# One group of products with v for each unit, and w2 loaded, measured and split by groups of its own

## The chip, the cores and the metric

The kernel runs on one NeuronCore of a Trainium2 chip. The metric is the time of one execution on the device in microseconds (us), and a kernel's time is the median over its runs. Beside it stands the profile of one execution: every instruction of TensorE (PE, with its weight loads as PEld), VectorE (DVE), ScalarE (ACT), GpSimd (POOL) and of the queue on SyncE that issues the DMAs (SP), with start, length and what released it.

## What is computed

A block of a transformer over 2048 tokens of width 512: a layer norm, then attention with a sliding window (32 heads of width 16, window 256) and beside it a SwiGLU network of inner width 1792; their product is added to the input. All inputs and the output are float32.

```python
B, S, D = 1, 2048, 512        # H = 32, Dh = 16, W = 256, F = 1792
xn = _layernorm(x, axis=-1)

qkv = (xn @ wqkv).reshape(B, S, 3, H, Dh).transpose(2, 0, 3, 1, 4)
q, k, v = qkv[0], qkv[1], qkv[2]
scores = jnp.einsum("bhqd,bhkd->bhqk", q, k) * (Dh ** -0.5)
mask = (idx[:, None] - idx[None, :] >= 0) & (idx[:, None] - idx[None, :] < W)
p = _softmax(jnp.where(mask[None, None], scores, -1e9), axis=-1)
o = jnp.einsum("bhqk,bhkd->bhqd", p, v)
s = o.transpose(0, 2, 1, 3).reshape(B, S, D) @ wo

h = _silu(xn @ w1) * (xn @ w3)
g = _silu(h @ w2)
return x + s * g
```

## The kernel before

**Precision.** Large products run in float16, each float32 operand split into a high and a low half after a scaling by powers of two, so that one product is three matmuls (high by high, high by low, low by high). Each weight is measured first: sums of squares by rows on ACT or DVE (`squares`, L222), a small matmul with ones that sums them over the partitions, and some ten small DVE instructions that turn the sum into a power of two (`powers`, L250). Then `split_pool` (L302) makes the halves: ACT scales the raw tile in place (L303) and casts the high half (L304), POOL subtracts twice for the low half (L300).

**Tiles.** The tokens are cut into four tiles `t` of 512. The attention of a tile is done for four groups `g` of eight heads, each in two passes `p`: 32 **units** (t, g, p). The network of a tile runs over 14 blocks `f` of 128 inner columns: `gate_up` (products with w1 and w3, L836) and, after each of the four groups of blocks in `GROUPS` (f 0 to 3, 4 to 7, 8 to 10, 11 to 13), `down` (products with w2, L881). The weights are split during tile 0 and written to DRAM (`dW1`, `dW2`), from where the later tiles load them.

**A unit.** A first pass over a unit's scores (`pass1`, L588), made two units ahead, gives the row maxima: VectorE reads each pair of score tiles with its mask and keeps the maximum (the `junk` instructions, L600). Call one such row M if its scores lie in one of the two double banks of the pool `pss` (tile `s`), and X if they lie in `po`, the one double bank of the pool `pso`. The second pass (`pass2`) makes the scores once more, turned, in five chunks (four in tile 0): a W row is one chunk's score matmuls into `s` (L662), DVE adds the mask (L669), ACT takes the exponential into a float32 tile `pt` (L672). The products of `pt` with v (L690, called V here) gather all chunks in `po`; at the unit's end ACT copies one half of `po` to `os` (L700) and DVE adds the other (L703), and only then is `po` free for the next X.

**Order.** TensorE's order is the order in which the code is written; on the other engines a scheduler sets the order by priorities, and each engine takes its list in order. `PLAN` and `FIRST_PLAN` (L1020, L1021) give a unit's five batches of rows: "WMX" is a W, an M and an X row, and the numbers behind it are the chunks whose products with v follow. `spread` (L1052) puts the dense matmuls (network, projections) between the batches, by their cost in matmuls of 512 columns; a chunk's products with v count `COLS` = 2.5. `later(n, f)` makes `f` n steps on, a step being a batch or a piece of some six dense matmuls; `beside_scores` hangs a small product onto one of the next M or X rows.

**Slots.** Raw weights, halves and the tiles of the network live in 41 slots of 2 KB per partition, which `take` and `give` hand round, the longest free first. In tile 0 `load(0, f)` (L762 to L766) loads w1, w3 and w2 of a block together, five blocks ahead (`LEAD`); `measure` (L770) takes two blocks with their six tiles at once; `measure_down` (L803) at a group's end only combines the powers already found (`p132`) and lets `cut` split the raw w2 tiles, which have lain in their slots since.

Of the kernel before, what the change touches and what calls it, by code (L numbers as in the profile page):

```python
# [10 lines left out]
F32 = mybir.dt.float32  # L11
BF16 = mybir.dt.bfloat16
# [9 lines left out]
P = 128  # L22
# [29 lines left out]
SLOTS = 41  # L52
# [26 lines left out]
def tile_block(ctx: ExitStack, tc: tile.TileContext, x, wqkv, wo, w1, w3, w2, out):  # L79
# [15 lines left out]
    ppool = pool("ppool", 4)  # L95
# [656 lines left out]
    p132 = const.tile([P, FB], F32, name="p132")  # L752
    down_scale = const.tile([P, len(GROUPS)], F32, name="dsc")

    def load(t, f):
        if t:
            WF[t, f] = a, b = [take(F16) for _ in range(2)], take(F16)
            for k in range(2):
                nc.sync.dma_start(a[k], dW1[f, k])
            nc.sync.dma_start(b, dW2[f])  # L760
            return
        RAW[f] = raw, raw2 = [take(F32) for _ in range(2)], take(F32)  # L762
        for k, w in enumerate((w1, w3)):
            nc.sync.dma_start(raw[k].rearrange("p (c f) -> p c f", f=P),
                              w[:, f * P:(f + 1) * P].rearrange("(c p) f -> p c f", p=P))
        nc.sync.dma_start(raw2, w2[f * P:(f + 1) * P, :])  # L766
# [3 lines left out]
    def measure(f, apart=0):  # L770

        raws = [RAW[f + i][0] for i in range(2)]
        sb = squares([raws[0][0], raws[1][0], raws[0][1], raws[1][1], RAW[f][1], RAW[f + 1][1]], on_act=6 if f > 2 else 4, apart=apart)

        def scale(s=None):
            pp = small.tile([P, 3, 2], F32, name="pp")
            pi = small.tile([P, 3, 2], F32, name="pi")
            return then(s, powers(sb, 6, pp.rearrange("p a b -> p (a b)"), pi.rearrange("p a b -> p (a b)"), s),
                        lambda: rest(pp, pi))

        def rest(pp, pi):
# [21 lines left out]
    def measure_down(k):  # L803

        f0, f1 = GROUPS[k]
        n = f1 - f0
        q = small.tile([P, 1], F32, name="q")
        nc.vector.tensor_reduce(q, p132[:, f0:f1], axis=AX.X, op=ALU.max)
        nc.vector.tensor_scalar(down_scale[:, k:k + 1], q, 1.0 / (HS * WS), None, op0=ALU.mult)
        nc.vector.reciprocal(q, q)  # L810
        sw = small.tile([P, 4], F32, name="sw2")
        nc.vector.tensor_scalar(sw[:, 0:n], p13[:, f0:f1], q, WS, op0=ALU.mult, op1=ALU.mult)

        def cut(f):
            raw2 = RAW.pop(f)[1]
            WF[0, f][1] = b = take(F16)
            split_pool(b[:, 0:D], b[:, D:], raw2, sw[:, f - f0:f - f0 + 1])
            give(raw2, after=5)
        assert measured >= set(range(f0, f1))
        for i, f in enumerate(range(f0, f1)):  # L820
            later(1 + 2 * i, lambda f=f: cut(f))
# [137 lines left out]
    def feed_forward():  # L959
# [3 lines left out]
        for t in range(NT):  # L963
            for f in range(FB):
                if t == 0:
                    if f % 2 or f == 0:
                        pieces += [(0, lambda f=f: load(0, f)) for f in (range(f + LEAD, min(f + LEAD + 2, FB)) if f else range(4, LEAD + 1))]
# [275 lines left out]
```

## Time and profile before

| | |
|---|---|
| runs shown | 861.09, 861.37, 858.77 us; median 861.09 |
| the profiled execution: its own time | 861.01 us |
| the profiled execution: span from first to last instruction | 859.2 us |
| busy: DVE, ACT, POOL | 608.3 us (71%), 407.9 us (47%), 198.0 us (23%) |
| granted TensorE clock, mean over the span | 0.992 |

The busy time of an engine is the time in which at least one of its instructions ran. In a timeline a row gives start, length, engine, source line, operation, what is written and read, and a count; the bracket at the end tells how long the engine was idle ahead of it and what ended the wait. In the list of waits the three numbers are the total, the count and the longest.

### The profile page before, as it was taken

Reading aid. Unit: us, or ns where it says so; the run is one execution under the profiler, and the core shown is the slowest. Engines: PE = TensorE matmul, PEld = TensorE weight load, DVE = VectorE, ACT = ScalarE, POOL = GpSimd, SP = SyncE. Lnnn points to the kernel's source line nnn. Section 1 sums busy time; section 2 is a strip of 40 time slices with the busy share of each in tenths; the row PEclk is TensorE's granted clock in tenths of the full one; section 3 lists DMA queues with packets and bytes.
Section 4 is the critical chain, followed back from the end, with each engine's and each line's share of the span. In section 5 each row is a group of like instructions: output and inputs, shape, how many; then the busy total and the mean of one; then the engine's idle time right before and its main releaser. Section 6 shows DMA issues by size and latency. Waiting matters only on the chain.

```text
span 859.2 us, 22511 instructions
## 1 busy us (share of the span) xinstructions
PE 820.9 (96%) x8734; PEld 380.0 (44%) x8734; DVE 608.3 (71%) x2013; ACT 407.9 (47%) x598; POOL 198.0 (23%) x325
## 2 busy tenths in 40 slices
PE   9899888899999999998999999999999999999998
PEld 4344334444444444443444444444444444444444
DVE  8786656976787667797777876677676787675435
ACT  6898776273426444344343445443443444433521
POOL 2254256151113203111111112120211113031211
PEclk9999899999999999999999999999999999999999
DMA  9958446236643443452533432534442353333201
GB/s 303 292 195 258 144 143 183 74 101 193 174 121 89 116 118 110 147 151 64 132 104 86 144 104 80 164 118 106 143 128 89 102 153 84 112 102 90 62 13 59
DMA packets 95323, 110.62 MB, mean 129 GB/s; under 512 B 17200, under 2 KB 60528, under 8 KB 95216
## 3 DMA queue, kind: packets, MB, share of 16 engines
q1 hardware_dynamic: 94928, 108.67, 43.5%
q8 instruction: 68, 1.11, 0.6%
q10 hardware_dynamic: 288, 0.52, 0.2%
q14 instruction: 39, 0.32, 0.1%
HBM read 76.28 MB, written 28.57 MB: 122 GB/s over the span
## 4 chain that ended last, share of the span: by engine, by line
PE 57%; DVE 15%; issue 7%; DMA 7%; ACT 7%; POOL 4%; SPq 3%; DVEq 0%; POOLq 0%; ACTq 0%
PE m L836 20%; PE m L881 12%; PE po L690 6%; PE m L534 6%; DVE junk L600 5%; PE m L923 3%; POOL slot L300 3%; PE s L662 3%; PE m L504 3%; DVE s L669 2%; PE s L588 2%; ACT pt L672 1%; DMA slot<-in_A_x_dram 1%; DMA dr<-dd 1%; SPq L734 1%
## 5 line engine op out<-in xcount | busy, mean ns | idle before, releaser
L300 POOL TENSOR_TENSOR slot<-slot,slot 128x256 f16<-128x256 f32 (+1 forms) x228 | 149.5, 681 | 568.1 <-ACT slot L860 446.2
L836 PE MATMUL m<-XH,slot 128*128 128x512 f16 x896 | 267.5, 380 | 2.7 <-DVE slot L851 1.9
L672 ACT ACTIVATE pt<-s,es 128x1024 f32<-128x1024 f32 x152 | 167.8, 1113 | 198.9 <-DVE s L669 186.4
L836 PEld LDWEIGHTS <-slot 128*128 128x128 f16 x1344 | 125.1, 98 | 158.5 <-issue 16.3
L836 PE MATMUL m<-XL,slot 128*128 128x512 f16 x448 | 169.8, 379 | 0.0
L881 PE MATMUL m<-slot,slot 128*128 128x512 f16 x672 | 159.5, 387 | 3.1 <-DVE slot L851 1.9
L600 DVE CUSTOM_DVE_ANT_0 junk<-s,MW 128x320 bf16<-128x320 f32 x288 | 139.6, 485 | 30.8 <-PE s L588 20.1
L669 DVE TENSOR_TENSOR s<-s,MK 128x256 f32<-128x256 f32 (+2 forms) x280 | 118.8, 434 | 55.3 <-PE s L662 51.1
L881 PEld LDWEIGHTS <-slot 128*128 128x128 f16 x672 | 63.1, 99 | 84.0 <-issue 14.4
L690 PE MATMUL po<-pt,V 64*32 64x320 f32 (+4 forms) x2880 | 84.8, 345 | 1.3 <-ACT pt L672 1.1
L600 DVE CUSTOM_DVE_ANT_0 junk<-po,MW 128x320 bf16<-128x320 f32 x160 | 77.3, 483 | 6.7 <-DVE M L600 0.5
L860 ACT CAST slot<-slot 128x512 f16<-128x512 f32 x56 | 34.6, 618 | 74.9 <-DVE slot L856 72.8
L851 DVE SCALAR_TENSOR_TENSOR slot<-slot,m 128x512 f32<-128x512 f32 x56 | 38.4, 685 | 32.1 <-ACT slot L847 32.0
L690 PEld LDWEIGHTS po<-pt,V 64*32 64x32 f32 x2880 | 47.1, 106 | 30.8 <-issue 5.5
L662 PE MATMUL s<-qa,KA 50*64 50x320 f16 (+3 forms) x1472 | 58.0, 259 | 1.7 <-ACT pt L672 0.9
L847 ACT ACTIVATE slot<-m,sgs 128x512 f32<-128x512 f32 x56 | 38.3, 683 | 41.8 <-PE m L836 39.7
L662 PEld LDWEIGHTS <-KA 50*64 50x64 f16 x1472 | 32.6, 105 | 56.4 <-issue 36.1
L588 PE MATMUL s<-KA,qa 48*64 48x320 f16 (+2 forms) x648 | 46.5, 299 | 6.5 <-DVE M L600 3.6
L856 DVE SCALAR_TENSOR_TENSOR slot<-m,slot 128x512 f32<-128x512 f32 x56 | 38.4, 686 | 17.9 <-PE m L836 17.3
L897 DVE SCALAR_TENSOR_TENSOR slot<-m,dsc,slot 128x512 f32<-128x512 f32 x48 | 35.7, 745 | 20.0 <-PE m L881 19.9
L588 PEld LDWEIGHTS <-qa 48*64 48x64 f16 x1024 | 29.6, 106 | 39.8 <-issue 26.6
L534 PE MATMUL m<-XH,whi 128*128 128x512 f16 x120 | 45.5, 387 | 1.6 <-DVE slot L897 0.9
(151 smaller groups left out, 880.7 us busy)
## 6 DMA issues: line engine op xcount, KB each, us to landing
slot<-dW SPq DMA_DIRECT2D x126, 256.0 KB
slot<-in_B_w_dram SPq DMA_DIRECT2D x42, 256.0 KB
dW<-slot SPq DMA_DIRECT2D x42, 256.0 KB
slot<-in_A_x_dram SPq DMA_DIRECT2D x30, 256.0 KB
KA<-dK SPq DMA_DIRECT2D x24, 288.0 KB
qa<-dQ SPq DMA_DIRECT2D x32, 192.0 KB
dK<-slot SPq DMA_DIRECT2D x16, 256.0 KB
dQ<-slot SPq DMA_DIRECT2D x16, 256.0 KB
```

Of the source, the lines that this page charges most:

```text
L300: op(out[:, c], a[:, c], b[:, c])
L534: nc.tensor.matmul(cell["pp"], a[:, k, c, :], b[:, c, :], start=(c, i) == parts[0][0], stop=(c, i) == parts[-1][-1])
L588: nc.tensor.matmul(s[64 * c:64 * c + 64, r, :n], qa[rows, 2 * p + a, ii * P + 64 * c:ii * P + 64 * c + 64], ka[rows, 2 * p + a, e - n:e], ...
L600: nc.vector.tensor_tensor_reduce(out=junk[:, :n], in0=s[:, r, :n], in1=mask, scale=1.0, scalar=NEG, op0=ALU.add, op1=ALU.max, accum_out=M[ ...
L662: nc.tensor.matmul(s[64 * h:64 * h + 64, r, o:o + 64 * n], ka[rows, 2 * p + a, 64 * (m + 4):64 * (m + 5)], qa[rows, 2 * p + a, 64 * (m + k ...
L669: nc.vector.tensor_add(v, v, MK[:, kind, of:of + n, :].unsqueeze(1).to_broadcast([P, 2 * len(which), n, 64]))
L672: nc.scalar.activation(pt, s, AF.Exp, scale=es)
L690: nc.tensor.matmul(cell["po"][32 * i:32 * i + 32, h, 64 * (m + k):64 * (m + k + n)], V[64 * h:64 * h + 64, (4 * t + m // 2) % VB, hd * VW: ...
L836: nc.tensor.matmul(cell[k], w[:, (a * NC + c) * P:(a * NC + c + 1) * P], b[:, c, :], start=c == 0 and i == 0, stop=c == NC - 1 and i == 2)
L851: nc.vector.scalar_tensor_tensor(sg, sg, 1.0, cell[0], op0=ALU.add, op1=ALU.mult)
L856: nc.vector.scalar_tensor_tensor(sg, cell[1], 0.5 * HS / (WS * XS)**2, sg, op0=ALU.mult, op1=ALU.mult)
L881: nc.tensor.matmul(ps, hh[:, a * TW + b * P:a * TW + (b + 1) * P], w[:, c * D:(c + 1) * D], start=f == f0 and i == 0, stop=f == f1 - 1 and ...
```

## The change

1. **The plans.** All products with v of a unit now stand in its fifth batch. The X rows move from the first three batches to the second, third and fourth, the two W rows of one batch from the third to the fourth. As all five `pt` tiles live until then, their pool gets a fifth buffer, and `SLOTS` falls from 41 to 39.
2. **w2 in tile 0.** `load` takes w1 and w3 alone. w2 has its own `load_down`, two blocks ahead of the block that is being computed, and `measure_down` is called for each block: ACT squares the raw tile (L814), and with the last block of a group follow the cast, the small matmuls beside a row of scores, the powers and the cuts. `measure` now has four tiles instead of six. Of the first two pairs of blocks two squares each go to DVE as before, now those of w3.

```diff
-SLOTS = 41
+SLOTS = 39
-    ppool = pool("ppool", 4)
+    ppool = pool("ppool", 5)
...
-        RAW[f] = raw, raw2 = [take(F32) for _ in range(2)], take(F32)
+        RAW[f] = raw = [take(F32) for _ in range(2)]
...
-        nc.sync.dma_start(raw2, w2[f * P:(f + 1) * P, :])
...
-        sb = squares([raws[0][0], raws[1][0], raws[0][1], raws[1][1], RAW[f][1], RAW[f + 1][1]], on_act=6 if f > 2 else 4, apart=apart)
+        sb = squares([raws[0][0], raws[1][0], raws[0][1], raws[1][1]], on_act=4 if f > 2 else 2, apart=apart)
...
-            nc.vector.tensor_mul(p132[:, ff], p13[:, ff], pp[:, 2, :])
...
+    def load_down(f):
+        RAW2[f] = raw = take(F32)
+        nc.sync.dma_start(raw, w2[f * P:(f + 1) * P, :])
+
+    def measure_down(k, f):
...
+        nc.scalar.activation(sq, RAW2[f], AF.Square, accum_out=NORMS[k][:, f - f0:f - f0 + 1])
+        if f < f1 - 1:
+            return
+        sb = small.tile([P, n], BF16, name="sb2")
+        nc.vector.tensor_copy(sb, NORMS[k])
...
+            return then(s, powers(sb, n, p2, small.tile([P, n], F32, name="pi2"), s), lambda: rest(p2))
...
+            for i, f in enumerate(range(f0, f1)):
+                later(1 + 2 * i, lambda f=f: cut(f))
+        beside_scores(2, scale)
...
-                    pieces += [(0, lambda k=k: measure_down(k)) for k, (_, f1) in enumerate(GROUPS) if f == f1 - 1]
+                    pieces += [(0, lambda f=f: load_down(f)) for f in range(f + 2 if f else 0, min(f + 3, FB))]
+                    for m in range(f + 1 if f else 0, min(f + 2, FB)):
+                        k = next(k for k, (_, f1) in enumerate(GROUPS) if m < f1)
+                        pieces.append((0, lambda k=k, m=m: later(2, lambda: measure_down(k, m))))
...
-    FIRST_PLAN = (("WMX", ()), ("WMX", ()), ("WMX", ()), ("WM", (0, 1)), ("M", (2, 3)))
-    PLAN = (("WMX", ()), ("WMX", ()), ("WWX", ()), ("WM", (0, 1, 2)), ("MM", (3, 4)))
+    FIRST_PLAN = (("WM", ()), ("WMX", ()), ("WMX", ()), ("WMX", ()), ("M", (0, 1, 2, 3)))
+    PLAN = (("WM", ()), ("WMX", ()), ("WMX", ()), ("WWX", ()), ("MM", (0, 1, 2, 3, 4)))
...
-    LAST_PLANS = ((("LW", ()), ("WW", ()), ("WW", (0, 1, 2)), ("", (3, 4))),
-                  (("WW", ()), ("WW", ()), ("W", (0, 1, 2)), ("", (3, 4))))
+    LAST_PLANS = ((("LW", ()), ("WW", ()), ("WW", ()), ("", (0, 1, 2, 3, 4))),
+                  (("WW", ()), ("WW", ()), ("W", ()), ("", (0, 1, 2, 3, 4))))
```

What this does to the order of instructions is shown at three places. The first is **TensorE in the fourth batch of the unit (t, g, p) = (1, 2, 0)**; `pt_5703` and `pt_5779` are the second and third of its five chunks (each of the rows stands there twice and is shown once). Before, dense matmuls (L504, values for the next tile) follow the third chunk:

```order
L690 MATMUL po_5875<-pt_5703,V_139 32x320 x2
L690 MATMUL po_5875<-pt_5779,V_139 32x320 x2
L690 MATMUL po_5875<-pt_5703,V_139 32x192 x2
L690 MATMUL po_5875<-pt_5779,V_139 32x192 x2
L504 LDWEIGHTS XH_3565
L504 MATMUL m1_5900<-wvh_466,XH_3565 128x512
```

Of the change, the same unit in its fifth batch; `pt_5742` and `pt_5826` are now the second and third chunk, `pt_5903` and `pt_5920` the fourth and fifth:

```order
L690 MATMUL po_5983<-pt_5742,V_139 32x320 x2
L690 MATMUL po_5983<-pt_5826,V_139 32x320 x2
L690 MATMUL po_5983<-pt_5742,V_139 32x192 x2
L690 MATMUL po_5983<-pt_5826,V_139 32x192 x2
L690 MATMUL po_5983<-pt_5903,V_139 32x320 x2
L690 MATMUL po_5983<-pt_5920,V_139 32x320 x2
```

The dense matmuls between the two groups have moved ahead of the first; the matmuls of V themselves and their order are the same.

The second place is **VectorE from the end of that unit**: L703 is the addition that frees `po`, and the first `junk` that reads `po` behind it belongs to the next unit's first X row (rows that only read out the accumulator are left out). Before:

```order
L703 TENSOR_TENSOR os_5966<-os_5966,po_5875 128x512
L927 SCALAR_TENSOR_TENSOR slot24_5977<-m0_5976,us_4192,slot24_5977 128x512
L669 TENSOR_TENSOR s_5997<-s_5997,MK_119 128x4x2x64
L600 ISA junk_6014,M_5996<-s_6009,MW_111 128x320
L600 ISA junk_6016,M_5996<-s_6009,MW_111 128x320
L600 ISA junk_6025,M_5996<-po_6018,MW_111 128x320
```

Of the change:

```order
L703 TENSOR_TENSOR os_6032<-os_6032,po_5983 128x512
L947 SCALAR_TENSOR_TENSOR slot25_5954<-m0_5953,us_4227,slot25_5954 128x512
L669 TENSOR_TENSOR s_6053<-s_6053,MK_119 128x4x2x64
L600 ISA junk_6070,M_6052<-s_6065,MW_111 128x320
L600 ISA junk_6072,M_6052<-s_6065,MW_111 128x320
L547 SCALAR_TENSOR_TENSOR slot9_6092<-m1_6079,slot9_6092 128x512
L669 TENSOR_TENSOR s_6108<-s_6108,MK_119 128x4x64
L600 ISA junk_6128,M_6052<-s_6121,MW_111 128x320
L669 TENSOR_TENSOR s_6108<-s_6108,MK_119 128x2x2x64
L600 ISA junk_6130,M_6052<-s_6121,MW_111 128x320
L621 CAST mt_6132<-s_6121 32x128
L600 ISA junk_6143,M_6052<-po_6138,MW_111 128x320
```

A whole batch (a W and an M row, with its dense matmuls) now lies between the freeing of `po` and the next row that needs it. On TensorE the dense matmuls between V and the next X were 12 for most units (9 to 15 over all); now there are 6 (3 to 9), the batch "WM" and 15 or 18 more. Between the batch "WWX" and the next rows, which need the banks of its two W rows, there were 12 in ten of the 22 units that have such a batch (15 to 24 in the others); now there are 18 in 19 of them (15, 21 and 24 in the others).

The third place is **ScalarE around the end of the first unit, (0, 0, 0)**. L231 are squares of w1 and w3, L814 (L231 with six tiles before) those of w2, L894 and L914 the first evictions of `down`, L700 the copy that frees `po`. Before:

```order
L231 ACTIVATE sqa_1975,ssq_1909<-slot18_1583 128x512
L700 COPY os_1486<-po_1408 128x512
L303 ACTIVATE slot38_745<-slot38_745,sw2_1915 128x512
L231 ACTIVATE sqa_1990,ssq_1909<-slot13_1589 128x512
L303 ACTIVATE slot5_751<-slot5_751,sw2_1915 128x512
L894 ACTIVATE slot3_1509<-m1_1496,dsc_156 128x512
L231 ACTIVATE sqa_2002,ssq_1909<-slot25_1584 128x512
L303 ACTIVATE slot8_828<-slot8_828,sw2_1915 128x512
L672 ACTIVATE pt_1535<-s_1522,es0_355 128x1024
```

Of the change:

```order
L814 ACTIVATE sqa_1632,ssq2_1172<-slot22_1260 128x512
L231 ACTIVATE sqa_1643,ssq_1576<-slot28_1096 128x512
L231 ACTIVATE sqa_1653,ssq_1576<-slot19_1100 128x512
L814 ACTIVATE sqa_1787,ssq2_1172<-slot12_1578 128x512
L231 ACTIVATE sqa_1974,ssq_1924<-slot30_1568 128x512
L700 COPY os_1495<-po_1458 128x512
L231 ACTIVATE sqa_1984,ssq_1924<-slot9_1572 128x512
L814 ACTIVATE sqa_1987,ssq2_1986<-slot8_1722 128x512
L914 ACTIVATE slot36_1511<-m1_1440,dsc_155 128x512
L231 ACTIVATE sqa_2004,ssq_1924<-slot17_1569 128x512
L672 ACTIVATE pt_1537<-s_1524,es0_346 128x1024
```

The splits of w2's second group (L303 with `sw2`) have gone from here to a later place, and squares whose tiles come by DMA stand closer together ahead of the copy, the eviction and the next exponential.

More of the change, by code (lines that the diff above doesn't have):

```diff
@@ L751, in tile_block @@
     p13 = const.tile([P, FB], F32, name="p13")
-    p132 = const.tile([P, FB], F32, name="p132")
     down_scale = const.tile([P, len(GROUPS)], F32, name="dsc")
@@ L765, in load @@
                               w[:, f * P:(f + 1) * P].rearrange("(c p) f -> p c f", p=P))
-        nc.sync.dma_start(raw2, w2[f * P:(f + 1) * P, :])
     measured = set()
     def measure(f, apart=0):
-        raws = [RAW[f + i][0] for i in range(2)]
-        sb = squares([raws[0][0], raws[1][0], raws[0][1], raws[1][1], RAW[f][1], RAW[f + 1][1]], on_act=6 if f > 2 else 4, apart=apart)
+        raws = [RAW.pop(f + i) for i in range(2)]
+        sb = squares([raws[0][0], raws[1][0], raws[0][1], raws[1][1]], on_act=4 if f > 2 else 2, apart=apart)
         def scale(s=None):
-            pp = small.tile([P, 3, 2], F32, name="pp")
-            pi = small.tile([P, 3, 2], F32, name="pi")
-            return then(s, powers(sb, 6, pp.rearrange("p a b -> p (a b)"), pi.rearrange("p a b -> p (a b)"), s),
+            pp = small.tile([P, 2, 2], F32, name="pp")
+            pi = small.tile([P, 2, 2], F32, name="pi")
+            return then(s, powers(sb, 4, pp.rearrange("p a b -> p (a b)"), pi.rearrange("p a b -> p (a b)"), s),
                         lambda: rest(pp, pi))
@@ L801, in measure, with scale, rest, cut @@
             later(10 if apart else 6, scale)
-    def measure_down(k):
+    RAW2 = {}
+    NORMS = {}
+    def load_down(f):
+        RAW2[f] = raw = take(F32)
+        nc.sync.dma_start(raw, w2[f * P:(f + 1) * P, :])
+    def measure_down(k, f):
         f0, f1 = GROUPS[k]
         n = f1 - f0
[L807 to L821, printed above, removed]
+        if f == f0:
+            NORMS[k] = small.tile([P, n], F32, name="ssq2")
+        sq = ppool.tile([P, D], BF16, name="sqa", bufs=1)
+        nc.scalar.activation(sq, RAW2[f], AF.Square, accum_out=NORMS[k][:, f - f0:f - f0 + 1])
[3 more added lines that the diff above has]
+        nc.vector.tensor_copy(sb, NORMS[k])
+        def scale(s):
+            p2 = small.tile([P, n], F32, name="pp2")
+            return then(s, powers(sb, n, p2, small.tile([P, n], F32, name="pi2"), s), lambda: rest(p2))
+        def rest(p2):
+            assert measured >= set(range(f0, f1))
+            nc.vector.tensor_mul(p2, p2, p13[:, f0:f1])
+            q = small.tile([P, 1], F32, name="q")
+            nc.vector.tensor_reduce(q, p2, axis=AX.X, op=ALU.max)
+            nc.vector.tensor_scalar(down_scale[:, k:k + 1], q, 1.0 / (HS * WS), None, op0=ALU.mult)
+            nc.vector.reciprocal(q, q)
+            sw = small.tile([P, 4], F32, name="sw2")
+            nc.vector.tensor_scalar(sw[:, 0:n], p13[:, f0:f1], q, WS, op0=ALU.mult, op1=ALU.mult)
+            def cut(f):
+                raw = RAW2.pop(f)
+                WF.setdefault((0, f), [[None, None], None])[1] = b = take(F16)
+                split_pool(b[:, 0:D], b[:, D:], raw, sw[:, f - f0:f - f0 + 1])
+                give(raw, after=5)
+            for i, f in enumerate(range(f0, f1)):
+                later(1 + 2 * i, lambda f=f: cut(f))
+        beside_scores(2, scale)
@@ L965, in feed_forward @@
                 if t == 0:
[L966 to L967 removed]
+                    if (f % 2 or f == 0) and f + LEAD < FB - 2:
+                        pieces += [(0, lambda f=f: load(0, f)) for f in (range(f + LEAD, f + LEAD + 2) if f else range(4, LEAD + 1))]
+                    elif f + LEAD == FB - 1:
+                        pieces += [(0, lambda f=f: load(0, f)) for f in range(FB - 2, FB)]
                     if f % 2 and f + 3 < FB:
                         pieces.append((0, lambda f=f + 3: measure(f, 1)))
[L970 removed]
+                    pieces += [(0, lambda f=f: load_down(f)) for f in range(f + 2 if f else 0, min(f + 3, FB))]
+                    for m in range(f + 1 if f else 0, min(f + 2, FB)):
+                        k = next(k for k, (_, f1) in enumerate(GROUPS) if m < f1)
+                        pieces.append((0, lambda k=k, m=m: later(2, lambda: measure_down(k, m))))
                 else:
```

2 lines of the change are left out of this document (1 added, 1 removed).

## The prediction

> **What bounds the kernel now.** First the page's busy times, then the windows that cut the span into long stretches, with the granted clock in the third column from the end.
>
> ```profile
> span 859.2 us, 22511 instructions
> PE 820.9 (96%) x8734; PEld 380.0 (44%) x8734; DVE 608.3 (71%) x2013; ACT 407.9 (47%) x598; POOL 198.0 (23%) x325
> ```
>
> ```profile
> 94.10:100.90 6.80, 6.17 (x24) 2.34 (x25) 2.55 (x14) 4.47 (x10) 0.01 (x1) 0.50 0.40 138
> 152.10:155.50 3.40, 3.40 (x10) 1.20 (x9) 3.40 (x13) 1.00 (x1) 0.00 (x0) 0.50 0.18 44
> 391.00:394.40 3.40, 3.40 (x10) 1.21 (x8) 2.45 (x10) 1.11 (x1) 1.24 (x2) 0.50 0.25 72
> 200.00:400.00 200.00, 193.49 (x2158) 89.70 (x2159) 149.10 (x494) 82.64 (x105) 35.87 (x54) 0.99 0.46 129
> 400.00:600.00 200.00, 197.01 (x2360) 92.68 (x2362) 145.39 (x462) 83.39 (x102) 33.29 (x50) 1.00 0.41 114
> 600.00:800.00 200.00, 197.46 (x2194) 91.11 (x2187) 139.17 (x436) 83.47 (x101) 35.95 (x54) 1.00 0.38 110
> ```
>
> TensorE is the bound: busy for 820.9 of 859.2 us, and for 588 of the 600 us from 200 to 800. Only three things can move the end much: its work, its 38 us of idle time, and the three stretches in which it was granted half the clock (6.8 + 3.4 + 3.4 us, so some 6.8 us lost). The idle time is uneven: 12 us between 200 and 800, and most of the rest in the first 200, where the weights are split. The list of waits, whole, then for the first 200 us, then for what follows, names what bears on this change:
>
> ```profile
> PE po L588 <- DVE os L703: 9.0, 8, 3.8
> PE s L588 <- ACT pt L672: 2.1, 5, 0.7
> PE po L690 <- ACT pt L672: 1.1, 1, 1.1
> ...
> PE po L588 <- DVE os L703: 5.9, 3, 3.8
> ...
> PE po L588 <- DVE os L703: 3.1, 5, 1.2
> ```
>
> The largest wait of all is an X row that needs `po` while the unit before it is still being copied out of it.
>
> **The products with v in one group.** The timeline of TensorE, rows of three places in units of tile 1, the third a view of the end of one group:
>
> ```profile
> 378.22 0.31 PE L588 MATMUL s<-KA,qa 48*64 48x320 f16 x4
> 378.46 1.53 PE L690 MATMUL po<-pt,V 64*32 64x256 f32 x48
> ...
> 401.18 0.31 PE L588 MATMUL po<-KA,qa 48*64 48x320 f16 x4
> 401.42 0.39 PE L836 MATMUL m<-XH,slot 128*128 128x512 f16 x1
> ...
> 405.69 0.53 PE L690 MATMUL po<-pt,V 64*32 64x192 f32 x16
> ...
> 405.86 0.37 PE L690 MATMUL po<-pt,V 64*32 64x192 f32 x8
> 406.16 0.39 PE L923 MATMUL m<-slot,slot 128*128 128x512 f16 x1
> ```
>
> From the last M row to V it takes 0.24 us from start to start, and from the last such row to a dense matmul 0.24 us as well. So the fourth batch, which loses its V, saves nothing at the front. It saves the way out: one pass of eight V matmuls follows the pass before it after 0.17 us, but a dense matmul follows the last pass after 0.30 us. Where V goes on into V, 0.13 us goes. That is once for each of 32 units: **-4.2 us**. The matmuls of V themselves are the same in number, size and order, so nothing else of their time changes. The lower bound of this term is nothing, if the next fetch of weights fills the gap again; the upper bound is the whole 0.30 us, 9.6 us. I take the measured difference.
>
> [...]
>
> **The wait for `po`.** How it arises, once in a quiet place and once in tile 0:
>
> ```profile
> 264.63 1.07 PE L690 MATMUL po<-pt,V 64*32 64x320 f32 x32
> ...
> 268.32 0.41 PE L662 MATMUL s<-qa,KA 50*64 50x256 f16 x8
> 268.56 0.31 PE L588 MATMUL s<-KA,qa 48*64 48x320 f16 x4
> 270.08 0.33 PE L588 MATMUL po<-KA,qa 48*64 48x320 f16 x4 [1.21 <-DVE os L703]
> ```
>
> ```profile
> 148.79 0.62 ACT L304 CAST slot<-slot 128x512 f16<-128x512 f32 x1 [2.65 <-POOL slot L300]
> 149.32 0.72 ACT L303 ACTIVATE slot<-slot,sw 128x512 f32<-128x512 f32 x1
> 149.94 0.56 ACT L700 COPY os<-po 128x512 f32<-128x512 f32 x1
> ```
>
> In the first, V starts at 264.63, and the X row could have started at about 268.87, that is 4.2 us later with 12 dense matmuls between; it had to wait to 270.08. In the second the copy out of `po` stood behind a cast that itself waited 2.65 us for POOL, and TensorE lost 3.8 us. After the change 6 dense matmuls, a batch "WM" and 18 more follow V. A dense matmul takes 0.22 us (401.42 and its like), so V's end to the next X grows from about 3.2 us to 24 x 0.22 + 2 x 0.6 = 6.5 us, by 3.3 us. The longest of these eight waits is 3.8 us, the next 1.4. I count all eight as gone: **-9.0 us**. What comes late next at these places is the W or M row of the same batch, which waits for its bank in `s`; it does not need `po`. The lower bound is what the part from 200 us on holds, 3.1 us, if each wait of the first 200 us is taken over by another engine's lateness.
>
> **The rows behind two W rows.** The five waits of an M row for the exponential look like this:
>
> ```profile
> 282.36 0.42 PE L662 MATMUL s<-qa,KA 50*64 50x320 f16 x12
> 283.12 0.33 PE L588 MATMUL s<-KA,qa 48*64 48x320 f16 x4 [0.34 <-ACT pt L672]
> ```
>
> The M row takes over the bank of the second of two W rows a batch earlier, 12 dense matmuls (2.6 us) away. Now 18 lie there in nearly all units, 1.3 us more than before, and no wait of this kind was longer than 0.7 us: **-1.9 us** of the 2.1. V itself needs the fifth exponential one batch later than its scores, as before.
>
> **The clock.** Two of the three stretches at half clock start right behind a wait for `po`: that at 152.1 behind the one of 3.8 us, that at 391.0 behind one of 0.7 us which closes a row of three. Without them the clock should stay: 3.4 x 0.5 for each, **-3.4 us**. The first, at 94.1, follows a wait of 2.9 us for a maximum (L600), and I leave it in.
>
> [...]
>
> **w2 on its own.** The work is the same: as many squares, casts and subtractions, the same DMAs. On ACT it is the groups
>
> ```profile
> L231 ACT ACTIVATE sqa<-slot 128x512 bf16<-128x512 f32 x48 | 30.1, 628 | 6.0 <-DMA slot<-in_B_w_dram 4.7 <-DMA slot<-in_A_wqkv_dram 0.9
> L304 ACT CAST slot<-slot 128x512 f16<-128x512 f32 x46 | 27.2, 614 | 4.5 <-POOL slot L300 3.0 <-PE m L881 1.0 <-PE s L662 0.3
> ```
>
> with the same counts. What is added: four groups of small matmuls beside a row of scores, and about ten small DVE instructions for each, less the seven multiplications that go.
>
> ```profile
> 60.78 0.18 PE L263 MATMUL s<-sb,onesb 64*64 64x6 bf16 x4
> 60.81 0.31 PE L588 MATMUL s<-KA,qa 48*64 48x320 f16 x4
> ...
> L275 DVE TENSOR_SCALAR al<-al 128x6 int32<-128x6 int32 (+1 forms) x13 | 2.6, 197 | 0.1
> ```
>
> The next row of scores starts 0.03 us behind such a group of four, so TensorE pays 0.1 us, **+0.2** with the entry. DVE pays 4 x 10 x 0.2 - 7 x 0.2 = 6.6 us, spread over 180 us in which it is busy about 70% of the time; its idle time hides it, and without that cover all 6.6 would show. What is moved is the danger: a square stands in ACT's list ahead of evictions and exponentials, and ACT takes its list in order. One case is in the trace:
>
> ```profile
> 114.42 0.63 ACT L231 ACTIVATE sqa<-slot 128x512 bf16<-128x512 f32 x1 [3.81 <-DMA slot<-in_B_w_dram]
> ...
> 115.05 1.09 ACT L672 ACTIVATE pt<-s,es 128x1024 f32<-128x1024 f32 x1
> ...
> 116.20 1.05 PE L690 MATMUL po<-pt,V 64*32 64x320 f32 x28 [1.09 <-ACT pt L672]
> ```
>
> ACT waited 3.8 us for a weight, the exponential behind it came late, TensorE lost 1.1 us. Now ten of the fourteen w2 tiles (f 4 to 13) are loaded about one and a half blocks ahead of their square, some 8 us by 24 dense matmuls a block, and queue on SP behind writes of split weights that wait for POOL. In the third place of the order shown, seven such squares stand ahead of an eviction that TensorE's next bank waits for. Against that, the loads at the start are fewer by a third, and w2 no longer holds its slots from five blocks ahead, so that w1 and w3 come earlier. The bounds are from a gain of 1.1 us (the old case gone) to ten times 1.1 us; near to the one row there is, two such stalls of about 1.1 us: **+2.3 us**. The fifth `pt` buffer and the two slots fewer I cost at nothing: tiles 1 to 3 load two blocks ahead, about 10 us.
>
> **The sum** is made against the profiled execution's own time, 861.0 us (its span, and 1.8 us around it), which is within 0.1 us of the median of the runs shown, 861.1: 861.0 - 4.2 - 9.0 - 1.9 - 3.4 + 0.2 + 2.3 = **845.0 us**.
>
> **The rivals.**
>
> *The first 200 us give it back.* There DVE, ACT and POOL set the pace in turns, and TensorE, let go at one place, stops at the next: the list above has `po` waiting for `os` with 5.9 us there, but also the 2.9 us wait for a maximum. Then the 5.9 us and the stretch at 152.1 stay: 845.0 + 5.9 + 1.7 = 852.6 us. For it speaks that the longest wait came from POOL, which keeps its work; against it that the waits go away by 3.3 us of distance, whoever causes them.
>
> *Nothing is gained.* V now needs the last two exponentials at once, and the row behind it follows sooner (6 dense matmuls). If TensorE waits 0.35 us for `pt` in each of 24 units, 8.4 us more come to 852.6: 861.0 us. For it speaks that such waits of 0.2 to 0.7 us exist; against it that they arise behind 12 dense matmuls and now have 18.
>
> *Slower: ACT held by w2.* If each of the ten late tiles stops ACT for 3.8 us as in the row above, and TensorE, which takes up the freed `s` and `m` banks within about 1 us, loses 2.8 of it, that is 28 us, and two more drops of the clock, 3.4: 845.0 - 2.3 + 31.4 = 874 us. It decides from about 1.8 us of loss for each tile, where the 18 us of the other terms are used up. Against it: in the trace ACT waited only twice for a weight, 4.7 us in all, though w2 then queued in the same list.
>
> [...]
>
> **How the numbers follow.** The unknown terms at their low ends (9.6 us for V, 1.1 us gained on w2) give 845.0 - 5.4 - 3.4 = 836.2 us, at their high ends (nothing for V, 11 us lost on w2) 845.0 + 4.2 + 8.7 = 857.9. All of them at one end is unlikely, so the forecast's own range is 838 to 851, and it has 0.62. The first rival, 851 to 857, has 0.21; the second, within 0.3% (2.6 us, about what a measurement of this kernel can tell from no change), 0.08; the third 0.09. So faster 0.83, same 0.08, slower 0.09. The range from 837 to 857 leaves out the last two, 0.17, and a little below.
>
> **What would show it.** In the profile after, "PE po <- DVE os" should be gone from the list of waits, and "PE s <- ACT pt" with it but for some tenths. V should stand in one row of about 2.5 us in each unit of tiles 1 to 3, against 1.46 and 1.19. TensorE's busy time should fall by about 4 us and half of the clock's 3.4, its idle time to about 29 us. The windows from 200 to 800 should have at most 7 us of idle time. If I am wrong, ACT's list will show L814 waiting for DMAs by more than 5 us, or the first `down` of tile 0 waiting for its w2 halves, or the half clock will be granted at new places.

## The result, and the profile after

The changed kernel takes **838.58 us** (median of 4 runs, 837.43 to 839.88) against 860.56 us for the kernel before, measured beside it: a ratio of 0.975, 95% interval 0.972 to 0.977. The forecast was 845.0 us, its range 837 to 857. The direction and the range held; the time is 6.4 us below the forecast.

The page of the profiled execution (its own time 837.43 us), and the windows of the changed kernel with the granted clock in the third column from the end:

```profile
span 835.6 us, 22584 instructions
PE 809.6 (97%) x8750; PEld 381.5 (46%) x8750; DVE 614.4 (74%) x2034; ACT 408.2 (49%) x598; POOL 196.7 (24%) x325
```

```profile
200.00:400.00 200.00, 196.73 (x2300) 93.67 (x2299) 156.08 (x514) 89.65 (x116) 42.27 (x64) 1.00 0.46 135
400.00:600.00 200.00, 199.56 (x2306) 94.65 (x2304) 149.66 (x473) 85.08 (x105) 34.75 (x53) 1.00 0.43 119
600.00:800.00 200.00, 199.24 (x2285) 93.66 (x2289) 137.69 (x413) 85.24 (x104) 38.42 (x58) 1.00 0.36 102
92.30:95.70 3.40, 3.40 (x9) 1.21 (x8) 2.05 (x11) 3.34 (x7) 0.00 (x0) 0.50 0.44 156
```

The span is 23.6 us shorter. Of that, TensorE's busy time gave 11.3 us (820.9 to 809.6) and its idle time 12.3 us (38.3 to 26.0). From 200 to 800 us only 4.5 us of idle time are left, from 12.0. One stretch at half clock remains, the last row.

The list of waits of the changed kernel, its head; `po <- os` is nowhere in it:

```profile
PE s L588 <- DVE M L600: 4.0, 2, 2.9
PE m L856 <- DVE slot L547: 2.5, 3, 1.3
PE po L588 <- DVE XL L472: 1.9, 2, 1.1
PE s L588 <- ACT pt L672: 1.9, 3, 0.7
```

### The profile page after: what moved, and what is told of

The parts are those of the page before. It is cut to its first block, busy times and chain, and to the rows that moved or that the text cites. A ratio compares the mean times of both kernels' runs of the same rounds, so it can differ in the third digit from the quotient of the medians.

```text
span 835.6 us, 22584 instructions
## 1 busy us (share of the span) xinstructions
PE 809.6 (97%) x8750; PEld 381.5 (46%) x8750; DVE 614.4 (74%) x2034; ACT 408.2 (49%) x598; POOL 196.7 (24%) x325
## 4 chain that ended last, share of the span: by engine, by line
PE 68%; DVE 9%; issue 7%; DMA 6%; ACT 5%; POOL 3%; SPq 2%; POOLq 0%; ACTq 0%; DVEq 0%
PE m L856 24%; PE m L901 13%; PE po L690 8%; PE m L534 6%; PE s L662 5%; PE m L943 4%; PE m L504 3%; POOL slot L300 3%; DVE junk L600 2%; PE s L588 2%; DMA slot<-in_B_w_dram 2%; DMA qa<-dQ 1%; DVE s L669 1%; PE po L588 1%; ACT slot L303 1%
## 5 line engine op out<-in xcount | busy, mean ns | idle before, releaser
L856 PEld LDWEIGHTS <-slot 128*128 128x128 f16 x1344 | 124.8, 98 | 159.9 <-issue 17.7
L600 DVE CUSTOM_DVE_ANT_0 junk<-s,MW 128x320 bf16<-128x320 f32 x276 | 134.3, 486 | 24.7 <-PE s L588 15.7
L901 PEld LDWEIGHTS <-slot 128*128 128x128 f16 x672 | 62.5, 98 | 82.2 <-issue 12.3
L600 DVE CUSTOM_DVE_ANT_0 junk<-po,MW 128x320 bf16<-128x320 f32 x172 | 83.7, 487 | 5.6 <-DVE al L272 0.4
L690 PE MATMUL po<-pt,V 64*32 64x320 f32 (+4 forms) x2880 | 77.7, 343 | 0.5 <-DVE pp L277 0.5
L690 PEld LDWEIGHTS po<-pt,V 64*32 64x32 f32 x2880 | 51.9, 106 | 24.1 <-PE s L588 4.7
L871 DVE SCALAR_TENSOR_TENSOR slot<-slot,m 128x512 f32<-128x512 f32 x56 | 38.3, 684 | 28.0 <-ACT slot L867 27.0
L662 PEld LDWEIGHTS <-KA 50*64 50x64 f16 x1472 | 30.2, 105 | 55.7 <-issue 36.1
L876 DVE SCALAR_TENSOR_TENSOR slot<-m,slot 128x512 f32<-128x512 f32 x56 | 38.5, 688 | 12.3 <-PE m L856 11.4
L534 PE MATMUL m<-XL,whi 128*128 128x512 f16 x120 | 44.5, 379 | 0.0
```

Source lines behind the costliest of these rows:

```text
L534: nc.tensor.matmul(cell["pp"], a[:, k, c, :], b[:, c, :], start=(c, i) == parts[0][0], stop=(c, i) == parts[-1][-1])
L600: nc.vector.tensor_tensor_reduce(out=junk[:, :n], in0=s[:, r, :n], in1=mask, scale=1.0, scalar=NEG, op0=ALU.add, op1=ALU.max, accum_out=M[ ...
L662: nc.tensor.matmul(s[64 * h:64 * h + 64, r, o:o + 64 * n], ka[rows, 2 * p + a, 64 * (m + 4):64 * (m + 5)], qa[rows, 2 * p + a, 64 * (m + k ...
L690: nc.tensor.matmul(cell["po"][32 * i:32 * i + 32, h, 64 * (m + k):64 * (m + k + n)], V[64 * h:64 * h + 64, (4 * t + m // 2) % VB, hd * VW: ...
L856: nc.tensor.matmul(cell[k], w[:, (a * NC + c) * P:(a * NC + c + 1) * P], b[:, c, :], start=c == 0 and i == 0, stop=c == NC - 1 and i == 2)
L876: nc.vector.scalar_tensor_tensor(sg, cell[1], 0.5 * HS / (WS * XS)**2, sg, op0=ALU.mult, op1=ALU.mult)
```

## The experiments

All times are medians beside the kernel before on the same chip; the ratio is to that kernel. "The change" means the changed kernel. The profiled executions took their medians within 2 us, but for that of e4 (847.87 against 844.91).

### The two parts apart

**e1, the plans alone.** From the kernel before: the new plans, the fifth `pt`, 39 slots.

```diff
-SLOTS = 41
+SLOTS = 39
-    ppool = pool("ppool", 4)
+    ppool = pool("ppool", 5)
-    FIRST_PLAN = (("WMX", ()), ("WMX", ()), ("WMX", ()), ("WM", (0, 1)), ("M", (2, 3)))
+    FIRST_PLAN = (("WM", ()), ("WMX", ()), ("WMX", ()), ("WMX", ()), ("M", (0, 1, 2, 3)))
...
```

> The new plans (all products with v in the fifth batch, X rows in batches two to four), the fifth pt buffer and the 39 slots, with w2 loaded, measured and split as before the change. If the plans carry the whole gain and w2 on its own costs the 2.3 to 2.5 us that the forecast gave it: about 836 us. If w2 on its own is worth something, because w1 and w3 come earlier and three waits of the first 200 us (1.98, 1.85 and 1.09 us, at 40.7, 79.4 and 116.2 in the trace before) went with it: about 843.5 us, with a wait of ACT for the loads of 3 us or more and at least one of the three TensorE waits back. If w2 does nothing either way: 838.6 within 1.3 us. In all three 'po <- os' is gone and PE's idle time from 200 to 800 us is 4 to 6 us.

**e2, w2 alone.** The change with the plans and the four `pt` buffers of before.

```diff
-    ppool = pool("ppool", 5)
+    ppool = pool("ppool", 4)
...
-    PLAN = (("WM", ()), ("WMX", ()), ("WMX", ()), ("WWX", ()), ("MM", (0, 1, 2, 3, 4)))
+    PLAN = (("WMX", ()), ("WMX", ()), ("WWX", ()), ("WM", (0, 1, 2)), ("MM", (3, 4)))
```

> The reverse: w2 on its own, the 39 slots, but the plans and the four pt buffers of before. If w2 costs what the forecast gave it: 863.5 us. If it is worth something: 856 to 858 us, with the wait for os still some 8 to 9 us in 8 to 9 places and all three half-clock stretches but perhaps one. If neither: 860.6 within 1.3 us. If the parts only work together, both this run and that of the plans alone stay within 5 us of before.

Measured: e1 **842.80 us** (0.980, 0.979 to 0.982), e2 **849.30 us** (0.988, 0.986 to 0.990). The plans bring 16.9 us, w2 on its own 10.4, and both together 22.0, which is 5.3 less than the sum: part of what they save is the same. So w2 on its own does not cost; beside the plans it brings 4.2 us. The list of waits of e1, its head:

```profile
PE s L588 <- DVE M L600: 3.7, 2, 2.7
PE s L258 <- DVE al L273: 2.0, 1, 2.0
PE s L662 <- DVE mt L621: 1.9, 1, 1.9
```

The first of the list of waits of e2:

```profile
PE po L588 <- DVE os L703: 7.1, 9, 1.3
```

The plans alone remove the wait for `os` entirely. With w2 alone it stays, as expected, but its longest case, the one behind ACT and POOL in the first 200 us, falls from 3.8 to 1.3 us. That e2 gained 10 us and not 3 was not expected by any of the theories. In its trace TensorE is idle for 30.8 us (847.5 - 816.7) against 38.3, and half clock is granted for 6.8 us against 13.6; which part of w2's own handling does it stays open.

### What the plans gain: distance and handovers

**e4, X rows early.** The change with the X rows in batches one to three again, so that they come 6 dense matmuls behind V.

```diff
-    PLAN = (("WM", ()), ("WMX", ()), ("WMX", ()), ("WWX", ()), ("MM", (0, 1, 2, 3, 4)))
+    PLAN = (("WMX", ()), ("WMX", ()), ("WWX", ()), ("WM", ()), ("MM", (0, 1, 2, 3, 4)))
```

> The changed kernel with the X rows moved back to batches one to three; all products with v stay in batch five, so only 6 dense matmuls lie between the last of them and the next X row: it could start about 2.0 us behind the last pass of V, against 6.46 us in the trace after. In that trace os is read out of po 1.6 us behind the last V in most units, but 2.1 to 6.7 us in about half of those up to 310 us and a few later ones. If the distance is what removed the wait for os: sum of the excess over 2.0 us about 20 us, nearly all in the first 320 us, so 855 to 860 us, and some half-clock stretches back. If the wait went for another reason (one copy instead of two groups of V, the w2 squares): 838.6 within 2.5 us.

Measured **844.91 us** (0.983, 0.982 to 0.984): 6.3 us more than the change, in the expected direction, though a third of the size. Its waits:

```profile
PE po L588 <- DVE os L703: 12.0, 11, 3.0
```

The wait is back, in 11 places, by distance. (The edit also puts the two W rows of one batch back into the third; the waits for the exponential stayed small, 1.2 us in all.) Why it costs nothing in the change is read from the timeline of one quiet unit of the changed kernel, TensorE first:

```profile
394.12 2.55 PE L690 MATMUL po<-pt,V 64*32 64x256 f32 x96
396.61 0.60 PE L856 MATMUL m<-XH,slot 128*128 128x512 f16 x2
...
402.86 0.32 PE L588 MATMUL po<-KA,qa 48*64 48x320 f16 x4
```

The two reads of `po` behind it, on ACT:

```profile
396.71 0.59 ACT L700 COPY os<-po 128x512 f32<-128x512 f32 x1 [3.77 <-PE po L690]
```

and on DVE:

```profile
397.33 0.69 DVE L703 TENSOR_TENSOR os<-os,po 128x512 f32<-128x512 f32 x1 [0.59 <-ACT os L700]
```

`po` is free at 398.0, 1.6 us behind the start of the last V matmul (396.4), and the X row comes at 402.86: 6.46 us behind that start, the distance that the prediction gave as 6.5. Over all units of the change, `po` was free after 1.6 us in the median and after 6.7 at worst.

**e3, a sixth batch.** The change with V in two groups behind all rows; chunks 3 and 4 in a batch of their own.

```diff
-    PLAN = (("WM", ()), ("WMX", ()), ("WMX", ()), ("WWX", ()), ("MM", (0, 1, 2, 3, 4)))
+    PLAN = (("WM", ()), ("WMX", ()), ("WMX", ()), ("WWX", ()), ("MM", (0, 1, 2)), ("", (3, 4)))
```

> The changed kernel, but with the products with v in two groups again, behind all rows: chunks 0 to 2 in batch five, 3 and 4 in a sixth batch without rows (tile 0: 0 and 1, then 2 and 3), so that dense matmuls stand between the groups. X rows stay where the change put them. If a group costs its two handovers (V to dense 0.30 against 0.17 us from pass to pass, dense to V 0.31 against 0.22 us start to start): 0.13 + 0.09 us in each of 32 units, 7 us, so 845 to 846 us; with the way out alone 4.2 us, 842.8 us. If the fetch of weights hides them: 838.6 us. The busy time of PE should carry the difference, its waits should not.

Measured **857.44 us** (0.998, 0.997 to 0.999): 18.9 us more, far above 845. A sixth batch also spreads the dense matmuls anew, and the waits for exponentials grew to 12.2 us, so the run does not isolate V.

**e6, two near groups.** As e3, but the positions of the five batches are kept: 6 of the dense matmuls ahead of V now stand between its groups, and no step is counted for the sixth batch.

```diff
...
+            goal = whole * (k + 1) / len(made)
+            if len(made) == 6:
+                goal = (whole / 5, 2 * whole / 5, 3 * whole / 5, 4 * whole / 5 - 6, 4 * whole / 5 + made[4][0], whole)[k]
```

> The changed kernel with the products with v split in two groups and nothing else moved: six of the dense matmuls that stand ahead of V in a unit now stand between chunks 0 to 2 and chunks 3 and 4 (tile 0: between 0, 1 and 2, 3), in the first 30 units. If a further group costs its two handovers, measured in the run with the sixth batch as 1.459 + 1.190 against 2.485 us on V and 0.309 against 0.214 us into it: 0.26 us in 22 units and about 0.13 in the 8 of tile 0, 6.8 us, so 845.4 us, and PE's busy time up by as much. If the 18.9 us of that run came from V in two groups as such, whatever stands between: 855 us or more. If only the way out counts: 842.5 us. If the fetch of weights hides it: 838.6 us.

Measured **857.26 us** (0.996, 0.995 to 0.998): 18.7 us more, not 6.8. The head of its list of waits, where the change has 1.9 us:

```profile
PE s L588 <- ACT pt L672: 9.6, 22, 0.8
```

One place ahead of V in its timeline of TensorE:

```profile
470.70 0.33 PE L588 MATMUL s<-KA,qa 48*64 48x320 f16 x4
470.86 0.40 PE L462 MATMUL s<-identf,slot 64*64 64x64 f32 x16
471.66 0.33 PE L588 MATMUL s<-KA,qa 48*64 48x320 f16 x4 [0.40 <-ACT pt L672]
472.05 1.53 PE L690 MATMUL po<-pt,V 64*32 64x256 f32 x48
...
474.91 1.26 PE L690 MATMUL po<-pt,V 64*32 64x320 f32 x48
```

The M rows now come 12 dense matmuls behind the two W rows in most of the 22 units with such a batch, not 18 (at this place 9), and an M row finds its bank of `s` still read by the exponential: 20 of the 22 waits in the list stand there. In the kernel before, 12 stood there in ten units, but a W row of the next batch came ahead of the M row (0.42 us in the prediction's rows), and five of the ten waited.

**e8, the last rows early.** V in one group; the M rows and V 6 dense matmuls earlier.

```diff
...
+            if len(made) == 5 and k == 3:
+                goal = goal - 6
```

> The changed kernel with the last batch of each unit, its M rows and all of V, 6 dense matmuls earlier: 12 in place of 18 between the two W rows of batch four and the M rows, 12 in place of 6 behind V. V stays in one group. The run with V in two near groups had these 12 as well, and in its trace an M row of that batch came 0.57 us late and the next 0.15 us, in 22 units. If that run's 18.7 us were 6.8 us of handovers and the rest this wait for the exponential: 857.3 - 6.8 = 850.5 us here, at most 854.5 (22 x 0.72 on 838.6), with 20 or more waits of 's <- pt'. If the 18.7 us came from splitting V alone: 838.6 within 1.5 us.

Measured **848.66 us** (0.987, 0.985 to 0.989), with this list:

```profile
PE s L588 <- ACT pt L672: 11.4, 22, 1.4
```

This separates e6: 10.1 us (848.66 - 838.58) come from the 12 dense matmuls in place of 18, and 8.6 us (857.26 - 848.66) from the split of V. The traces bear it out: TensorE was idle for 34.4 us in e6 and 34.7 in e8 against 26.0 in the change, and the split shows in the busy time, 821.3 against 811.6 us, of which 1.7 us is a further stretch at half clock. Over 30 units 8.6 us is 0.29 us for one more way out and way in; the rows give 0.16 (1.459 + 1.190 against 2.485 us) and 0.09 (0.309 against 0.214 us), 0.26 together in 22 units and less in tile 0, so 6.8 of the 8.6 us.

**e9, V at the very end.** All dense matmuls of a unit ahead of its last batch, so that the W row of the next unit follows V at once.

```diff
...
+            if len(made) == 5 and k == 3:
+                goal = whole
```

> The changed kernel with the 6 dense matmuls that stand behind V in a unit moved ahead of its last M rows, in 30 units, so that V is followed at once by the W row of the next unit. One way out of the tiles and one way in go from each unit: 0.13 us (V to dense 0.30, V to V 0.17) and 0.09 us (dense to W 0.31, dense to dense 0.21), 6.6 us, so 832 us by the handovers, with PE's busy time down by 6 to 7 us. The X row then comes 5.1 us behind V in place of 6.46, still above the 1.6 to 2.5 us that the copy out of po takes in most units; three of the first 200 us (6.7, 5.1 to 5.3) would wait up to 2 us in all. Rival: the W row wants its bank of s before DVE has taken the maxima of the M rows ahead of V, or the work of DVE and ACT bunches there: 0.2 us or more lost in each unit, 838 us or more.

Measured **845.14 us** (0.982, 0.980 to 0.984): the rival. Its timeline of TensorE behind V:

```profile
446.11 2.55 PE L690 MATMUL po<-pt,V 64*32 64x256 f32 x96
449.07 0.41 PE L662 MATMUL s<-qa,KA 50*64 50x256 f16 x8 [0.41 <-DVE XL L472]
```

The head of its list of waits:

```profile
PE s L662 <- DVE M L600: 5.4, 5, 2.0
PE s L588 <- DVE M L600: 5.1, 3, 4.1
PE s L662 <- ACT pt L672: 4.0, 6, 1.1
```

The W row finds its bank of `s` still in use: by the maxima on DVE in five cases, by the exponential in six, here by the cast of the next x tile (L472). TensorE was idle for 33.1 us (845.0 - 811.9) against 26.0, and half clock was granted for 13.6 us in place of 3.4, which loses 5.1 us more. So the 6 dense matmuls behind V have a use in the change: they give DVE and ACT time to empty `s`.

### What w2 on its own gains

**e5, w2 loaded early.** The change, but each w2 tile is loaded with the w1 and w3 tiles of its block; it is still measured and split on its own.

```diff
+        load_down(f)
...
-                    pieces += [(0, lambda f=f: load_down(f)) for f in range(f + 2 if f else 0, min(f + 3, FB))]
```

> The changed kernel with only the loads of w2 moved back: each w2 tile is loaded with the w1 and w3 tiles of its block again, five blocks ahead, while it is still measured and split on its own, group by group. The plans alone took 842.8 us, the whole change 838.6, so w2 on its own brings 4.2 us beside the plans. If that comes from the loads (fewer in SP's list ahead of x, w1 and w3 in the first 100 us): back to 842 to 843 us, with DVE's waits for loads of x and the TensorE waits of 1 to 2 us before 130 us back. If it comes from the measuring (four squares and four columns for a pair of blocks in place of six, no w2 squares on DVE at the start): 838.6 within 1.5 us. If, as the forecast had it, late loads cost 2.3 us: 836.3 us.

Measured **835.67 us** (0.971, 0.970 to 0.973). So the late loads cost 2.9 us, near the 2.3 of the forecast (the 95% intervals overlap at their edge, the runs themselves do not), and the gain lies elsewhere: 7.1 us from e1 to e5. Those two differ in the measuring of w2, in the place of its splits, and in one thing more, which is part of the change and so of every run here but e1:

```diff
...
+                    elif f + LEAD == FB - 1:
+                        pieces += [(0, lambda f=f: load(0, f)) for f in range(FB - 2, FB)]
```

The w1 and w3 tiles of the last two blocks are loaded one block later than before; these four loads are issued from 105 to 116 us in e1 and from 114 to 121 us in e5. Where e5 gains, shows the start of V in the same units of the four traces (us):

| unit | e1, plans alone | the change | e5 | e12 |
|---|---|---|---|---|
| 1 | 87.50 | 84.99 | 85.78 | 87.39 |
| 3 | 140.94 | 138.54 | 138.11 | 140.52 |
| 4 | 170.15 | 164.58 | 162.74 | 165.17 |
| 5 | 193.04 | 188.32 | 186.47 | 188.89 |
| 32 | 801.76 | 798.27 | 795.66 | 797.62 |

From e1 to e5 there are two steps: 1.7 us up to the first unit, and 4.6 us between the third and the fourth (2.8 to 7.4), with 1.1 between. Of it 6.1 us are left at the end. Of these, 5.1 us are lost to half clock: e1 was granted it for 3.4 us at 94.6 and 6.8 us at 156.0, e5 at neither place. Over all their runs the share is smaller: a granted clock of 0.9935 in the mean for e1 and 0.9974 for e5 makes some 3.3 of the 7.1 us, by estimate. In the first step stands the wait of 2.0 us for the powers (`s L258 <- al`). In the second step, e1 has the 1.9 us wait for `mt` and right behind it 6.8 us at half clock. TensorE's timeline there:

```profile
155.95 0.60 PE L662 MATMUL s<-qa,KA 50*64 50x320 f16 x10 [1.94 <-DVE mt L621]
```

Ahead of it the scores of a W row (150.47, with 0.41 us) waited for their mask on DVE, which first went through the 13 instructions for 1/std of the next x tile, from 150.05 on. One of them, and the mask behind them:

```profile
151.10 0.59 DVE L419 SCALAR_TENSOR_TENSOR sq<-sq,ve 128x4 f32<-128x4 f32 x1
...
154.67 0.43 DVE L669 TENSOR_TENSOR s<-s,MK 128x256 f32<-128x256 f32 x1
```

In the change the mask of that row stands in the middle of the chain (150.83 us, behind scores that start at 148.23), and TensorE waited 0.24 us for the same `mt`. The window behind the wait in e1, with the granted clock in the third column from the end:

```profile
156.00:162.90 6.90, 5.85 (x59) 3.00 (x60) 6.90 (x25) 2.52 (x3) 0.00 (x0) 0.51 0.12 43
```

**e12, squares at the start.** e5 with the squares of the first four w2 tiles on ACT behind those of the first pairs, ten there as before; the small matmuls for their powers are hung on a row of scores 14 steps on, in place of 2.

```diff
...
         measure(0)
+    for m in range(2):
+        measure_down(0, m)
...
     measure(2, 1)
+    for m in range(2, 4):
+        later(m, lambda m=m: measure_down(0, m))
```

> The kernel with all of w2 loaded early (835.7 us), with the squares of the first four w2 tiles put back to the start: on ACT, behind those of the first two pairs, so that ACT has ten squares there again in place of six; the powers of two of that group still come beside a score row later. Unit by unit, the plans alone were 1.7 to 2.5 us behind that kernel at the first V, and 4.6 us fell behind between the third unit and the fifth (138 to 193 us). If ten squares at the start make the wait of 2.0 us at 40.7 us (powers of the first pair): it comes back in part, 837 to 838 us. If that delay alone also set off the later loss: 842 to 843 us. If it was neither, but the w2 squares on DVE or the loads' order: 835.7 within 1.2 us.

Measured **836.74 us** (0.973, 0.972 to 0.974). In its trace the first step is back (1.6 us at unit 1, 2.4 at unit 4, 2.0 at the end), but not as the wait at 40.7 us: TensorE waits 1.4 us for a square on ACT at 31 to 32 us, and half clock at 34.6 us costs 1.7 us more. The 1.1 us between the medians lie within their intervals. The second step is not back: the start does not set it off. Which of the other differences does, the measuring of later blocks with six tiles, the place of the splits or the earlier loads of the last two blocks, no run isolates; the loads are an untested rival, issued some 35 to 50 us ahead of the wait for `mt`.

**e11, mixed.** e5 with the first four w2 tiles late.

```diff
+        if f > 3:
+            load_down(f)
...
+                    if f == 0:
+                        pieces += [(0, lambda m=m: load_down(m)) for m in range(4)]
```

> w2 loaded early (with w1 and w3, five blocks ahead) for the blocks from 4 on, but late, as in the change, for the first four. Unit by unit, the trace with all of w2 early is 0.8 us behind that of the change when the first V starts (85 us; two waits for qa, 1.4 and 0.7 us at 32 us, stand there), 1.9 us ahead after unit four, and 2.6 us ahead after unit seven. If the late loads cost only from block 4 on and the early ones only at the start: 835.7 - 0.8 = 834.9 us, with the two waits for qa gone. If the start's lead is taken back by a later wait, as elsewhere before 200 us: 835.7 us or more.

Measured **834.90 us** (0.971, 0.969 to 0.973), the number of the sum, and the wait for `qa` is down to 0.2 us. The lead of 0.8 us on e5 lies within the intervals of both; 3.7 us ahead of the change, it is the lowest median here.

**e10, e5 and e9 together.**

```diff
+        load_down(f)
...
+            if len(made) == 5 and k == 3:
+                goal = whole
```

> The two together: w2 loaded with w1 and w3 (835.7 us by itself) and V followed at once by the next unit's W row. If both terms stand and add: 829 us. If they take the same waits away: 832 us. If V at the end bunches work: 836 us or more.

Measured **846.37 us** (0.984, 0.982 to 0.986): V at the end loses again, 10.7 us against e5.

### The wait that is left

**e7, the chain for 1/std in parts.**

```diff
-            for i in range(3):
-                nc.vector.tensor_mul(sq, r0, r0)
...
+            for i in range(3):
+                if t:
+                    later(1 + i, lambda i=i: newton(i))
```

> The changed kernel, but the 13 small DVE instructions that make 1/std for the next x tile are issued in four parts, a step apart, and the four that centre x three steps later, so that the maxima of the score rows stand between them in DVE's list. In the trace after, that chain holds DVE from 83.9 to 90 us, TensorE waits 2.9 us for a maximum at 91.7 and gets half the clock for 3.4 us; a chain of the same kind costs 1.1 us at 376.8. If the chain is what is waited for: 2.9 + 1.1 + 1.7 us go, so about 833 us, with no half clock. If DVE is simply full there and the next thing in its list is late instead: 837 us or more, with a wait of 2 us or more still between 85 and 100 us.

Measured **839.51 us** (0.975, 0.973 to 0.978): no gain. The edit did not reach its aim: in DVE's list all 13 instructions still stood in a row, from 83.5 to 89.4 us, as the scheduler of that engine places them by priority, and the maxima came behind; the wait at 91.3 us was 2.7 us. Whether splitting the chain helps stays open.

## Why the prediction was right, and where it was wrong

- **V in one group, -4.2: right.** 0.164 us in each of the 24 units of tiles 1 to 3 (1.459 + 1.190 against 2.485 us) and 0.04 us in the 8 of tile 0 make 4.3. The 0.13 us that the prediction took for all 32 units was too little for the one kind and too much for the other; that the sum agrees so closely is luck. e6 against e8 puts 0.29 us on a split that has dense matmuls on both sides, which is above what the change saved, because the fourth batch had its rows ahead of V anyway.
- **The wait for `po`, -9.0: right.** All eight are gone, and e4 brings 12.0 us of such waits back by distance. In time, though, they cost e4 only 6.3 us. The first rival, by which the first 200 us give it back, happened in small part: the idle time there fell from 22.0 to 17.7 us, while waits for `po` of 5.9 us went.
- **The rows behind two W rows, -1.9: only from 200 us on.** There the 2.1 us went. Three new ones, 1.9 us, came in tile 0, where ACT and DVE carry the splits as well. The mechanism was right: with 12 dense matmuls in place of 18, e8 has 22 such waits. A loss of the second rival's size, 0.35 us in each unit, is about what e8 measured at that distance (10.1 us); at 18 it did not occur.
- **The clock, -3.4: too small.** Half clock fell from 13.6 to 3.4 us, worth 5.1 us. The first stretch shrank as well, from 6.8 to 3.4 us, though the wait ahead of it stayed at 2.9 us; what differed is a further 0.6 us of idle time in its first 3.4 us before, and none in the change.
- **w2, +2.3 (and +0.2): the step that failed.** The prediction said that the work is the same, and looked for the price of its new place only, not for what w2 had cost in its old one. The price of the late loads had the right size (2.9 us by e5), but not by the two stalls of TensorE behind ACT that it was worked out from, which the list of waits of the change does not show; in the two traces 1.7 us of it is the one stretch at half clock. Against it stand 7.1 us that the rest of w2's own handling gained, which the sum did not have. Without the two w2 terms the forecast is 842.5 us, and e1, the plans alone, took 842.8; the miss of 6.4 us is about this term, -4.2 where +2.5 stood. That e1 comes so close is in part luck: in its trace the clock saved 1.7 us in place of 3.4 and the waits for the exponential fell by 0.2 in place of 1.9, while the busy time fell by 8.7 us, where V and the clock make 6.0. The third rival, ACT held by w2, did not occur: ACT waited for w2 loads 3.2 us in all, by its list of waits:

```profile
ACT sqa L814 <- DMA slot<-in_B_w_dram: 3.2, 3, 2.3
```

- **The signs: the idle time nearly, the busy time not.** Idle time fell to 26.0 us, with 29 expected. Busy time fell by 11.3 us, where the prediction looked for 4 and half of the clock's 3.4. That halving is an error: a stretch of 3.4 us at half clock is 1.7 us too long (in that of the change a dense matmul starts 0.43 us behind the one before it, at full clock 0.22 us), so the 3.4 us for two stretches is busy time as a whole. With V at 4.3 and the clock at 5.1, a last 1.9 us has no explanation here.

## What to carry to other kernels

Moving a consumer to the end of its unit paid twice here, by a handover less (4.3 us) and by the distance that its buffer gains (waits of 9.0 us); but both ends of the distance count: 6 dense matmuls too few ahead cost 10.1 us here, and none behind in place of 6 cost 6.6 us, a saved handover and 5.1 us at half clock included. When work only changes its place, ask not only whom it may hold up in the new place but also whom it held up in the old one, and put a term of either sign into the sum. To find where two versions of a kernel part, compare the start of the same instruction, unit by unit, in both traces.

## What the runs showed of the hardware

**Half clock behind idle time of TensorE.** Half clock was granted to the kernel before at 94.1 us for 6.8 us and at 152.1 and 391.0 us for 3.4 us each, and to the change at 92.3 us for 3.4 us. In the 3.4 us ahead of these four stretches TensorE was idle for 2.9, 2.5, 1.8 and 2.8 us; at 391.0 that was in three waits of at most 0.8 us. In the first 3.4 us of the long stretch it was idle for 0.6 us more, in the three short ones not at all. Two waits of 2.9 us for a maximum had different ends. The change, where 3.4 us at half clock follow, in the timeline of TensorE:

```profile
91.71 0.25 PE L588 MATMUL s<-KA,qa 48*64 48x128 f16 x4 [2.92 <-DVE M L600]
```

The kernel e12, where none follow (its mean clock of 0.998 over 835.0 us is a loss of 1.7 us, which its stretch at 34.6 us accounts for):

```profile
94.12 0.25 PE L588 MATMUL s<-KA,qa 48*64 48x128 f16 x4 [2.94 <-DVE M L600]
```

**Small DVE instructions took longer beside POOL's subtractions.** DVE's timeline in the changed kernel:

```profile
85.86 0.60 DVE L419 SCALAR_TENSOR_TENSOR sq<-sq,ve 128x4 f32<-128x4 f32 x1
86.50 0.16 DVE L420 SCALAR_TENSOR_TENSOR r<-sq,r 128x4 f32<-128x4 f32 x1
86.70 0.16 DVE L418 TENSOR_TENSOR sq<-r 128x4 f32<-128x4 f32 x1
86.90 0.57 DVE L419 SCALAR_TENSOR_TENSOR sq<-sq,ve 128x4 f32<-128x4 f32 x1
```

POOL at the same time, four subtractions in each row:

```profile
83.88 2.57 POOL L300 TENSOR_TENSOR slot<-slot,slot 128x256 f16<-128x256 f32 x4 [2.02 <-ACT slot L304]
86.77 2.55 POOL L300 TENSOR_TENSOR slot<-slot,slot 128x256 f16<-128x256 f32 x4 [0.33 <-POOL slot L300]
```

In these rows an instruction on four elements for each partition took 0.16 us where it started in POOL's pause, and 0.57 to 0.60 us where it started beside a subtraction, of which one took 0.64 us (2.57 us for four). The chain that holds the maxima back at 91.7 us takes 6.1 us (83.68 to 89.74); eight of its 13 instructions, at 0.57 to 0.69 us each, start beside POOL's subtractions, and the other five, at 0.16 or 0.17 us, outside them, so some 3.5 us of it are this difference, by estimate.
